# Gate logits taken from the attention rows by transposes on the chip, with the output's zero blocks and half of a weight load placed later

## The chip, the cores and the metric

The kernel runs on one core of a Trainium2 chip. The metric is the device time of one execution in microseconds (us). The core has TensorE (PE, its weight loads shown apart as PEld), VectorE (DVE), ScalarE (ACT), GpSimd (POOL) and SyncE (SP); 16 DMA engines move data between DRAM and the on-chip memories.

## What is computed

Local attention (8 batches, 8 heads, 576 positions, head size 64, each position sees itself and the 63 before it) gives 4608 rows of 512 numbers. A top-2 mixture of 8 experts works on these rows.

```
scores = q @ k.T / 8, masked to 0 <= i - j < 64
attn = exp(scores - max) / sum;   x = attn @ v          # 4608 rows of 512
logits = x @ w_gate;  noise_scale = log1p(exp(x @ w_noise))
noisy = logits + noise_scale * noise                    # 8 numbers a row
top 2 of noisy per row, softmax over the two
out[row] += weight * (relu(x[row] @ w1[e]) @ w2[e])     # for both experts e
```

All is in 32 bit floats; large products are split into high and low parts (three matmuls for one product).

## The kernel before

**Attention units.** The rows are made in 36 units of 128 rows (j = 0 to 35: position block j // 4, batch pair j % 4). One loop of 39 turns (j = 0 to 38) writes out, in each turn, the steps of several units, since the steps of one unit follow each other over turns: `scores` of unit j (16 matmuls into ps_s), `soft_a`, `soft_max`, `soft_max2` (a copy on ACT, a predicated copy and a maximum on DVE, a subtraction on POOL), then for j-1 `soft_b` (the exponential, ACT), `transp` (4 transposes on PE into ps_t) and `apply_mask` (DVE, makes pt), for j-2 `pv` (32 matmuls, 16 in the first four units, into ps_o) and for j-3 `norm_a` and `norm_b` (ACT scales ps_o by the reciprocal sum and writes the rows x). `store` sends the rows of j-4 to DRAM. Each engine works its instructions strictly in the written order, and SP issues all of these DMAs from one list, waiting where a transfer's buffer is not yet free or its data not yet made.

**The gate's logits before.** A logit is linear in v, so the kernel multiplies v by the gate weights first: `load_vt` brings v of unit j transposed (tile vt), `logits` makes 4 matmuls of 64 columns into the bank ps_g, and `logits_copy` (two ACT instructions) puts the result beside v in the tile vw. `pv` then has 85 columns a matmul (5 groups of 17: four with 16 numbers of v each, one with the 16 logits of the head; the 17th column of the first group holds the ones that give the sum), and `gate` adds over the heads on DVE, once for two units.

**Routing.** When a group of units has its logits (`ROUTE`: units 0-6, 7-13, 14-20, 21-26, 27-35), the generator `route` yields some 45 small steps on DVE and ACT; `drain(n)` takes n of them at five places in a turn (`RATE`). `slots` holds further steps (DVE, POOL line 592, and `place`, small matmuls that write into ps_o or ps_g), taken by `drain_slots`. From turn `TURN` on, the first rows of expert 0, gathered by POOL, are transposed by PE (line 726) into ps_t and split.

**After the attention.** `up00` is the first product of expert 0; 16 of its steps (`AHEAD`) run inside the turns 36 to 38, the rest right after. From there on the experts follow, `up` and `down` for 15 chunks of rows; `add_rows` adds their results to the output in DRAM. The output's 38 blocks of zeros (`zero_out`, 256 KB each) must be written before. Some stand in the turns from `ZFROM` on (`blanks`, three a turn), some later. `load_w2(0, ...)` brings expert 0's second weights in four pieces of 512 KB; `split_w2` splits them.

## Time and profile before

| | |
|---|---|
| median of 3 runs | 1014.37 us (1011.97 to 1015.88) |
| the profiled execution's own time | 1015.99 us |
| its span, first to last instruction | 1014.3 us |
| PE busy | 968.3 us (95%) |
| DVE / ACT / POOL busy | 692.7 / 524.0 / 319.2 us |
| mean granted TensorE clock | 0.993 of full speed |

Times below are positions or lengths in us in that span. The scores of unit 0 begin at 5.69, those of unit 4 at 20.25, of unit 11 at 54.29, of unit 32 at 150.38, of unit 35 at 172.92; the last matmul of `up00` begins at 201.78, and the products after it run until the end. A busy share is no bound by itself: which wait ends last in a stretch tells what sets its length.

### The profile page before, as it was taken

Reading aid. Unit: us, or ns where it says so; the run is one execution under the profiler, and the core shown is the slowest. Engines: PE = TensorE matmul, PEld = TensorE weight load, DVE = VectorE, ACT = ScalarE, POOL = GpSimd, SP = SyncE. Lnnn points to the kernel's source line nnn. Section 1 sums busy time; section 2 is a strip of 40 time slices with the busy share of each in tenths; the row PEclk is TensorE's granted clock in tenths of the full one; section 3 lists DMA queues with packets and bytes.
Section 4 is the critical chain, followed back from the end, with each engine's and each line's share of the span. In section 5 each row is a group of like instructions: output and inputs, shape, how many; then the busy total and the mean of one; then the engine's idle time right before and its main releaser. Section 6 shows DMA issues by size and latency. Waiting matters only on the chain.

```text
span 1014.3 us, 22006 instructions
## 1 busy us (share of the span) xinstructions
PE 968.3 (95%) x8464; PEld 868.4 (86%) x8464; DVE 692.7 (68%) x1727; ACT 524.0 (52%) x1346; POOL 319.2 (31%) x442
## 2 busy tenths in 40 slices
PE   8788887999999999999999999999999999999995
PEld 8677786888889898989898989888998899889994
DVE  5589897663676678667766776777577766776630
ACT  4788785522354445444554455445454545455420
POOL 5346554122322414141414141404141414131202
PEclk9999998999999999999999999999999999999998
DMA  9999999557558544855584558545854685465303
GB/s 327 334 294 315 290 287 325 184 137 230 138 140 209 97 129 97 227 113 128 100 251 85 128 113 231 106 115 121 241 96 106 127 234 108 97 147 147 47 3 52
DMA packets 107234, 168.93 MB, mean 167 GB/s; under 512 B 13360, under 2 KB 57648, under 8 KB 105328
## 3 DMA queue, kind: packets, MB, share of 16 engines
q1 hardware_dynamic: 89968, 126.96, 40.8%
q0 software_dynamic: 17152, 40.48, 22.7%
q8 instruction: 68, 1.11, 0.5%
q14 instruction: 46, 0.38, 0.1%
HBM read 110.08 MB, written 57.32 MB: 165 GB/s over the span
## 4 chain that ended last, share of the span: by engine, by line
PE 81%; DVE 9%; ACT 3%; issue 3%; POOL 2%; DMA 1%; POOLq 0%; DVEq 0%; ACTq 0%
PE ps_d L1025 8%; PE ps_d L1023 8%; PE ps_d L1024 8%; PE ps_z L879 6%; PE ps_z L881 6%; PE ps_z L880 6%; PE ps_v L879 3%; PE ps_v L880 3%; PE ps_v L881 3%; PE ps_y L1023 3%; PE ps_y L1025 3%; PE ps_y L1024 3%; DVE pt L359 2%; PE ps_y L881 2%; PE ps_y L880 2%
## 5 line engine op out<-in xcount | busy, mean ns | idle before, releaser
L957 POOL DMA_INDIRECT out_dram<-xg,los x70 | 110.3, 1576 | 396.9 <-ACT xg L1036 364.1
L1025 PE MATMUL ps_d<-w2h,hb 128*128 128x512 f32 x392 | 153.4, 391 | 0.0
L1023 PE MATMUL ps_d<-w2h,hb 128*128 128x512 f32 x392 | 153.3, 391 | 0.0
L1024 PE MATMUL ps_d<-w2l,hb 128*128 128x512 f32 x392 | 153.0, 390 | 0.0
L891 ACT ACTIVATE hb<-tq 128x288 fp32r<-128x288 f32 (+1 forms) x168 | 77.1, 459 | 144.2 <-DVE tq L910 144.2
L910 DVE TENSOR_TENSOR tq<-ps_z,tq 128x288 f32<-128x288 f32 (+1 forms) x168 | 79.4, 472 | 88.3 <-PE ps_z L881 88.0
L879 PE MATMUL ps_z<-xh,WH 128*128 128x288 f32 (+1 forms) x448 | 137.4, 307 | 1.1 <-DVE tq L910 0.2
L881 PE MATMUL ps_z<-xh,WL 128*128 128x288 f32 (+1 forms) x448 | 135.1, 302 | 0.0
L880 PE MATMUL ps_z<-xl,WH 128*128 128x288 f32 (+1 forms) x448 | 135.1, 302 | 0.0
L895 DVE SCALAR_TENSOR_TENSOR hb<-tq,hb 128x320 fp32r<-128x320 f32 (+2 forms) x168 | 75.6, 450 | 37.6 <-ACT hb L891 35.3
L690 POOL DMA_INDIRECT xg<-xrows,lxs x70 | 69.9, 999 | 87.6 <-DMA xs<-xg 33.8
L879 PEld LDWEIGHTS ps_z<-xh,WH 128*128 128x128 f32 x448 | 84.1, 188 | 5.9 <-DVE tq L910 4.2
L1025 PEld LDWEIGHTS ps_d<-w2h,hb 128*128 128x128 f32 x392 | 73.6, 188 | 15.9
L1024 PEld LDWEIGHTS ps_d<-w2l,hb 128*128 128x128 f32 x392 | 73.6, 188 | 14.1
L1023 PEld LDWEIGHTS ps_d<-w2h,hb 128*128 128x128 f32 x392 | 73.6, 188 | 14.0
L880 PEld LDWEIGHTS ps_z<-xl,WH 128*128 128x128 f32 x448 | 84.2, 188 | 1.3
L881 PEld LDWEIGHTS ps_z<-xh,WL 128*128 128x128 f32 x448 | 84.2, 188 | 0.0
L235 DVE TENSOR_TENSOR WL<-ws,WH 128x512 fp32r<-128x512 f32 x112 | 67.1, 614 | 6.4 <-ACT WH L243 6.4
L399 ACT ACTIVATE x<-ps_o,r 128x80 f32<-128x80 f32 x288 | 66.8, 349 | 8.7 <-DVE r L389 8.6
L774 ACT ACTIVATE xh<-tq 128x512 fp32r<-128x512 f32 (+1 forms) x70 | 42.7, 610 | 53.4 <-DVE tq L770 51.3
L378 PE MATMUL ps_o<-vw,pt 64*64 64x85 f32 x2176 | 50.9, 237 | 17.6 <-issue 12.7
L378 PEld LDWEIGHTS ps_o<-vw,pt 64*64 64x64 f32 x2176 | 45.8, 135 | 22.4 <-issue 13.9
(241 smaller groups left out, 2377.5 us busy)
## 6 DMA issues: line engine op xcount, KB each, us to landing
ws<-in_w_dram SPq DMA_DIRECT2D x14, 2048.0 KB, 11.5
xs<-xg SPq DMA_DIRECT2D x63, 256.0 KB, 3.3
vw<-in_vx_dram SPq DMA_DIRECT2D x36, 272.0 KB, 4.7
out_dram<-zero SPq DMA_DIRECT2D x38, 256.0 KB, 5.7
qc<-in_qT_dram SPq DMA_DIRECT2D x36, 256.0 KB, 5.2
KW<-in_kT_dram SPq DMA_DIRECT2D x36, 256.0 KB, 5.0
vt<-in_vT_dram SPq DMA_DIRECT2D x36, 256.0 KB, 4.6
xrows<-x SPq DMA_DIRECT2D x36, 256.0 KB, 4.6
```

The costliest lines, as they stand in the source:

```text
L378: nc.tensor.matmul(PO[j][u * 64:u * 64 + 64, a, g * 2 + x, :], lhsT=pt[pa, w, u * 2 + g, x * 64:x * 64 + 64], rhs=v[pa, (i + w) % 2, :, u, ...
L690: nc.gpsimd.indirect_dma_start(out=XG[e, c, q][:m], out_offset=None, in_=X[:DUMP + seen.get((e, c), NT) * 128], in_offset=bass.IndirectOff ...
L879: nc.tensor.matmul(p[:, :n], lhsT=WH[:, a, k, w], rhs=xh[:, b, k, :n], start=first and k == 0, stop=False, **free)
L880: nc.tensor.matmul(p[:, :n], lhsT=WH[:, a, k, w], rhs=xl[:, b, k, :n], start=False, stop=False, **free)
L881: nc.tensor.matmul(p[:, :n], lhsT=WL[:, a, k, w], rhs=xh[:, b, k, :n], start=False, stop=(k == 1), **free)
L891: nc.scalar.activation(hh[:, f, a:b], src, AF.Relu)
L895: nc.vector.scalar_tensor_tensor(hl[:, f, a:m], src[:, :m - a], 0.0, hh[:, f, a:m].bitcast(F32), op0=OP.max, op1=OP.subtract)
L910: nc.vector.tensor_tensor(t, a[:, :n], t, op=OP.add)
L957: s = nc.gpsimd.indirect_dma_start(out=out[:(2 + seen.get((e, c), NT)) * 128], out_offset=bass.IndirectOffsetOnAxis(ap=LT[e, c][1][q][:m], ...
L1023: nc.tensor.matmul(p, lhsT=h, rhs=w2h[:, f, :], **a)
L1024: nc.tensor.matmul(p, lhsT=h, rhs=w2l[:, f, :], start=False, stop=False)
L1025: nc.tensor.matmul(p, lhsT=l, rhs=w2h[:, f, :], **b)
```

## The change

The logits are now made from the finished rows. `turn_rows` transposes the 512 numbers of each row of unit j-4 on PE (4 transposes of 128x128 into ps_g), `rows_copy` copies them by one ACT instruction to the new tile xq, and `logits` in the next turn makes 4 matmuls of 16 columns, one accumulation, into a free part of a ps_o bank; `gate` is a copy of 16 columns on DVE in each turn. The loads of vt, the line `logits_copy` and four POOL memsets of vw are gone; `pv` has 65 columns, and vw's load is 260 KB instead of 272 KB (the array of v is laid out anew by the host, with 64 numbers and a one for each head). `gate` comes two units later than before. For the last units a table (`LATE`) packs the remaining transposes and logits into turns 36 to 38 and behind the loop.

Zero blocks start at turn 36 instead of 32: 9 stand in the loop, 9 and 12 in the first `up` and `down` of expert 0, 8 in its second `up`. Expert 0's second weights are loaded in turns 35 to 38 instead of 34 to 37. `RATE` is 9 steps a turn instead of 8 and 7, `drain_slots` takes three a turn throughout, `TURN` is 33, and 14 steps of `up00` stand in the loop, 2 more behind it.

```diff
@@ -36,7 +36,7 @@
 W1G = 12
-TURN = 32
+TURN = 33
@@ -44,10 +44,10 @@
-ZFROM = 32
+ZFROM = 36
 HOLD = 4
-RATE = ((16, 8), (99, 7))
+RATE = ((99, 9),)
@@ -128,21 +128,13 @@
         i, bp = divmod(j, NP)
-        nc.sync.dma_start(VW[bp][:, i % 2, 0:4], vx[bp, i])
-    def load_vt(j):
-        i, bp = divmod(j, NP)
-        VT[j] = ld.tile([128, 4, 128], F32, name="vt", bufs=2)
-        nc.sync.dma_start(VT[j], vT[bp, i])
+        nc.sync.dma_start(VW[bp][:, i % 2], vx[bp, i])
         load_qk(j)
-    wgx_sb = acon.tile([128, 2, 64], F32)
+    wgx_sb = acon.tile([128, 4, 2 * E], F32)
     nc.sync.dma_start(wgx_sb, wgx)
-    load_vt(0)
     load_v(0)
-    load_vt(1)
@@ -181,8 +173,6 @@
     nc.vector.tensor_scalar(maskT[:, 1], maskT[:, 0], -1.0, 1.0, op0=OP.mult, op1=OP.add)
-    for v in VW:
-        nc.gpsimd.memset(v[:, :, 4], 0.0)
@@ -277,22 +267,22 @@
-    VG = idle[:, 0:256].rearrange("p (n c) -> p n c", n=1)
-    def logits(j):
-        p = VG[:, 0]
-        x = VT.pop(j)
-        for u in range(2):
-            for g in range(2):
-                q = u * 2 + g
-                nc.tensor.matmul(p[:, q * 64:q * 64 + 64], lhsT=x[:, q, :], rhs=wgx_sb[:, g], start=True, stop=True)
-    def logits_copy(j):
-        i, bp = divmod(j, NP)
-        for a in range(2):
-            h = slice(a * 64, a * 64 + 64)
-            nc.scalar.activation(VW[bp][h, i % 2, 4, :, :, 0:16].rearrange("p u (g x) e -> p (u g) x e", x=2),
-                                 VG[h, 0].rearrange("p (k a x e) -> p k a x e", a=2, x=2, e=16)[:, :, a], AF.Copy)
+    XQ, LP = {}, {}
+    def turn_rows(j):
+        x = XT[j]
+        for q in range(4):
+            nc.tensor.transpose(idle[:, q * 128:q * 128 + 128], x[:, q].rearrange("p h d -> p (h d)"), ident)
+    def rows_copy(j):
+        XQ[j] = wk.tile([128, 4, 128], F32, name="xq")
+        nc.scalar.activation(XQ[j], idle.rearrange("p (q t) -> p q t", q=4), AF.Copy)
+    def logits(j, o):
+        LP[j] = o[:, 0, 352 + j % 4 * 2 * E:352 + (j % 4 + 1) * 2 * E]
+        x = XQ.pop(j)
+        for q in range(4):
+            nc.tensor.matmul(LP[j], lhsT=x[:, q], rhs=wgx_sb[:, q], start=(q == 0), stop=(q == 3))
@@ -367,7 +357,7 @@
         OT[j] = o
-        PO[j] = o[:, :, 0:340].rearrange("p a (k d) -> p a k d", d=85)
+        PO[j] = o[:, :, 0:260].rearrange("p a (k d) -> p a k d", d=65)
@@ -377,7 +367,7 @@
                                              lhsT=pt[pa, w, u * 2 + g, x * 64:x * 64 + 64],
-                                             rhs=v[pa, (i + w) % 2, :, u, g * 2 + x, :],
+                                             rhs=v[pa, (i + w) % 2, u, g * 2 + x, :],
@@ -385,24 +375,24 @@
         RS[j] = r
-        nc.scalar.activation(r, PO[j][:, :, :, 16], AF.Copy, bias=1e-9)
+        nc.scalar.activation(r, PO[j][:, :, :, 64], AF.Copy, bias=1e-9)
             if j % 2 == 0:
-                XP[0] = wk.tile([128, 2, 5, H, 16], F32, name="x", bufs=2)
+                XP[0] = wk.tile([128, 2, 4, H, 16], F32, name="x", bufs=2)
             XT[j] = XP[0][:, j % 2]
-        o, r = PO[j][:, a].rearrange("p k (q d) -> p k q d", d=17), RS[j][:, a]
+        o, r = PO[j][:, a, :, 0:64].rearrange("p k (q d) -> p k q d", d=16), RS[j][:, a]
         for k in range(4):
-            nc.scalar.activation(XT[j][:, :, a * 4 + k], o[:, k, :, 0:16], AF.Copy, scale=r[:, k:k + 1])
+            nc.scalar.activation(XT[j][:, :, a * 4 + k], o[:, k], AF.Copy, scale=r[:, k:k + 1])
         nc.sync.dma_start(X[DUMP + j * 128:DUMP + (j + 1) * 128, :DM],
-                          XT.pop(j)[:, 0:4].rearrange("p q h d -> p (q h d)"))
-    LG, PG, held = {}, {}, []
+                          XT[j].rearrange("p q h d -> p (q h d)"))
+    LG, PG = {}, {}
@@ -410,12 +400,7 @@
             LG[c] = gw.tile([128, RT, 16], F32, name="lg", bufs=3)
-        held.append(j)
-        if j % 2 or j + 1 == ROUTE[c + 1]:
-            a = held[0] % 2
-            nc.vector.tensor_reduce(LG[c][:, held[0] - ROUTE[c]:j + 1 - ROUTE[c]],
-                                    XP[0][:, a:a + len(held), 4].rearrange("p n h e -> p n e h"), op=OP.add, axis=AX.X)
-            held.clear()
+        nc.vector.tensor_copy(LG[c][:, j - ROUTE[c]], LP.pop(j))
@@ -628,7 +613,7 @@
     def place_slots(j):
-        o = OT.pop(j)[:, 0, 340:340 + E * NQ]
+        o = OT[j][:, 0, 264:264 + E * NQ]
@@ -1069,7 +1054,7 @@
         for _ in range(n):
-            if j >= NT and len(taken) < AHEAD:
+            if j >= NT and len(taken) < AHEAD - (0 if kept else 2):
@@ -1089,6 +1074,9 @@
             zero_out()
+    kept = []
+    LATE = {NT: ([NT - 5], [NT - 4], []), NT + 1: ([], [NT - 3], [NT - 2]), NT + 2: ([NT - 2], [], [NT - 1])}
@@ -1101,8 +1089,8 @@
             load_v(j + 2)
-        if NT - 2 <= j < NT + 2:
-            load_w2(0, slice((j - NT + 2) * 2, (j - NT + 3) * 2))
+        if NT - 1 <= j < NT + 3:
+            load_w2(0, slice((j - NT + 1) * 2, (j - NT + 2) * 2))
@@ -1119,6 +1107,12 @@
         on(place_slots, j - 2)
+        ready = LATE[j][0] if j in LATE else [j - 5]
+        for k in ready:
+            on(logits, k, OT[min(j, NT + 1) - 2] if j > 1 else None)
+        if j == NT + 1:
+            turn_rows(j - 4)
+            rows_copy(j - 4)
@@ -1127,23 +1121,31 @@
             add_slots(placed.pop())
+        for k in ready:
+            on(gate, k)
         ahead(2)
-        on(logits, j)
-        if j < NT - 2:
-            load_vt(j + 2)
+        if j <= NT:
+            on(turn_rows, j - 4)
         drain(rate(2))
-        on(logits_copy, j)
+        if j <= NT:
+            on(rows_copy, j - 4)
         ahead(2)
-        on(gate, j - 3)
+        if j in LATE:
+            for k in LATE[j][1]:
+                logits(k, OT[min(j, NT + 1) - 2])
+                gate(k)
+            for k in LATE[j][2]:
+                turn_rows(k)
+                rows_copy(k)
         drain(rate(3))
-        drain_slots(2 if j >= DENSE else 1 + j % 2)
+        drain_slots(2)
@@ -1151,6 +1153,10 @@
     store(NT - 1)
+    kept.append(1)
+    ahead(2)
+    logits(NT - 1, OT[NT - 1])
+    gate(NT - 1)
@@ -1173,6 +1179,7 @@
             parts.append((0.0, 1.0, [lambda: drain_slots(1)] * 9))
+            parts.append((0.0, 0.8, [zero_out] * 9))
@@ -1218,6 +1225,7 @@
             parts.append((0.1, 0.96, [lambda: drain(2)] * 24))
+            parts.append((0.0, 0.9, [zero_out] * 12))
```

PE's list in a late turn, before (ps_s scores, vw v, ps_t transposed probabilities, vt transposed v, xg gathered rows of expert 0; the small matmuls of `place` are left out):

```order
L318 MATMUL ps_s<-KW,qc 64x128 x16
L378 MATMUL ps_o<-vw_93,pt 64x85 x32
...
L354 MATMUL ps_t<-ident,p 128x128 x4
L288 MATMUL ps_g<-wgx_sb,vt 128x64 x4
L726 MATMUL ps_t<-ident,xg 128x128 x4
```

Such a turn with the change (lines 275 and 285 are `turn_rows` and `logits`; x the finished rows, xq their transposed copy):

```order
L308 MATMUL ps_s<-KW,qc 64x128 x16
L368 MATMUL ps_o<-vw_90,pt 64x65 x32
...
L285 MATMUL ps_o<-wgx_sb,xq 128x16 x4
L344 MATMUL ps_t<-ident,p 128x128 x4
L275 MATMUL ps_g<-ident,x 128x128 x4
L711 MATMUL ps_t<-ident,xg 128x128 x4
```

The logits moved from behind the transposes of the probabilities to ahead of them, and four transposes of rows came in behind.

PE's list from the last `pv` on, before (WH, WL and xh are weights and rows of `up00`):

```order
L378 MATMUL ps_o<-vw_93,pt 64x85 x32
L836 MATMUL ps_t<-xh,WH 128x384
L837 MATMUL ps_t<-xl,WH 128x384
L838 MATMUL ps_t<-xh,WL 128x384
...
L608 MATMUL ps_g<-xc 128x80
```

With the change:

```order
L368 MATMUL ps_o<-vw_93,pt 64x65 x32
L275 MATMUL ps_g<-ident,x 128x128 x4
L821 MATMUL ps_t<-xh,WH 128x384
...
L285 MATMUL ps_o<-wgx_sb,xq 128x16 x4
L275 MATMUL ps_g<-ident,x 128x128 x4
L821 MATMUL ps_s<-xh,WH 128x384
```

Behind the last `pv` three more sets of transposes and three of logits now stand between the steps of `up00` (those of units 33, 34 and 35).

SP's list at the end of the attention, before (xrows<-x is `store`, xrows<-xc the gate weights of the last group, ws the staged expert weights):

```order
L219 DMA ws<-in_w_dram 128x1024
L199 DMA out_dram<-zero 256x1x256 x2
L402 DMA xrows<-x 128x512
L199 DMA out_dram<-zero 256x1x256 x3
L579 DMA xrows<-xc 128x9x16
L199 DMA out_dram<-zero 256x1x256 x8
L215 DMA ws<-in_w_dram 128x4096
L199 DMA out_dram<-zero 256x1x256 x9
```

With the change:

```order
L209 DMA ws<-in_w_dram 128x1024
L189 DMA out_dram<-zero 256x1x256 x2
L392 DMA xrows<-x 128x512
L189 DMA out_dram<-zero 256x1x256 x21
L564 DMA xrows<-xc 128x9x16
L189 DMA out_dram<-zero 256x1x256 x8
L205 DMA ws<-in_w_dram 128x4096
```

21 blocks now stand in a row behind the last store and ahead of the last gate weights.

## Rows read from the trace of the kernel before

**Rows 1.** Stretches of the span: length, busy time (instructions) of each engine, clock, DMA share, GB/s
```profile
0.00:20.25 20.25, 17.92 (x288) 16.67 (x288) 10.57 (x23) 6.61 (x19) 12.74 (x42) 1.00 0.90 315
20.25:54.29 34.04, 25.90 (x694) 23.78 (x693) 20.60 (x33) 27.73 (x104) 12.19 (x15) 1.00 0.99 337
54.29:150.38 96.09, 83.19 (x2323) 75.15 (x2322) 87.75 (x219) 79.23 (x304) 55.32 (x64) 1.00 0.94 295
150.38:172.92 22.54, 15.81 (x356) 14.11 (x356) 17.41 (x42) 12.58 (x46) 12.86 (x15) 0.93 1.03 359
172.92:201.95 29.03, 26.81 (x353) 25.21 (x352) 19.66 (x62) 16.93 (x58) 2.24 (x3) 0.94 0.55 184
201.95:1014.00 812.05, 798.66 (x4458) 713.50 (x4457) 536.76 (x1350) 380.89 (x819) 223.84 (x306) 1.00 0.58 135
```

**Rows 2.** The chain of work that ended last: start, length, what
```profile
2.28 1.06 POOL vw L185 x4
12.28 0.84 PE ps_g L288 x8
...
24.15 1.08 PE ps_s L318 x32
27.97 1.08 PE ps_s L318 x32
```

**Rows 3.** PE in order of time: start, length, instruction, count [idle before <- releaser]
```profile
13.05 0.69 PE L320 MATMUL ps_s<-KW,qc 64*64 64x64 f32 x32
13.56 0.81 PE L378 MATMUL ps_o<-vw,pt 64*64 64x85 f32 x32
...
35.05 1.11 PE L378 MATMUL ps_o<-vw,pt 64*64 64x85 f32 x48 [1.67 <-issue]
36.09 0.66 PE L354 MATMUL ps_t<-ident,p 128*128 128x128 f32 x4
36.58 1.00 PE L288 MATMUL ps_g<-wgx_sb,vt 128*128 128x64 f32 x8
37.51 1.10 PE L318 MATMUL ps_s<-KW,qc 64*64 64x128 f32 x32
38.44 0.89 PE L378 MATMUL ps_o<-vw,pt 64*64 64x85 f32 x35
40.65 0.81 PE L378 MATMUL ps_o<-vw,pt 64*64 64x85 f32 x29 [1.32 <-issue]
...
47.38 0.51 PE L378 MATMUL ps_o<-vw,pt 64*64 64x85 f32 x11 [2.44 <-issue]
```

**Rows 4.** DMA issues of the page: kind, count, size, median us to landing
```profile
out_dram<-zero SPq DMA_DIRECT2D x38, 256.0 KB, 5.7
vt<-in_vT_dram SPq DMA_DIRECT2D x36, 256.0 KB, 4.6
```

**Rows 5.** Groups of instructions between 54 and 150 us: count | busy, mean ns | idle before
```profile
L378 PE MATMUL ps_o<-vw,pt 64*64 64x85 f32 x1344 | 29.7, 235 | 7.6 <-issue 3.0 <-ACT t L328 1.7 <-DVE xc L539 1.0
L328 ACT ACTIVATE t<-ps_s 128x512 f32<-128x512 f32 x21 | 12.5, 594 | 4.4 <-PE ps_s L318 4.0 <-PE ps_g L469 0.4
L294 ACT ACTIVATE vw<-ps_g 64x128 f32<-64x128 f32 x42 | 11.5, 275 | 1.6 <-PE ps_g L288 1.3
L416 DVE TENSOR_REDUCE lg<-x 128x32 f32<-128x256 f32 (+1 forms) x13 | 6.5, 500 | 0.0
L389 DVE RECIPROCAL r<-r 128x8 f32<-128x8 f32 x21 | 4.1, 196 | 1.6 <-ACT r L388 1.6
L628 DVE TENSOR_TENSOR SLOT<-SLOT,ps_o 128x80 f32<-128x80 f32 x8 | 1.8, 227 | 0.0
```

**Rows 6.** PE in order of time, 150 to 184 us, columns as in the third group
```profile
157.53 0.66 PE L726 MATMUL ps_t<-ident,xg 128*128 128x128 f32 x4 [1.35 <-DVE pt L359]
...
169.03 0.37 PE L378 MATMUL ps_o<-vw,pt 64*64 64x85 f32 x6 [2.71 <-issue]
...
172.92 1.99 PE L318 MATMUL ps_s<-KW,qc 64*64 64x128 f32 x32
174.68 2.27 PE L378 MATMUL ps_o<-vw,pt 64*64 64x85 f32 x64
```

More of the change, by code (lines that the diff above doesn't have):

```diff
@@ L88, in tile_kernel @@
 @with_exitstack
-def tile_kernel(ctx, tc, qT, kT, vx, vT, wgx, noise, w1, w2, out):
+def tile_kernel(ctx, tc, qT, kT, vx, wgx, noise, w1, w2, out):
     nc = tc.nc
@@ L110, in tile_kernel @@
     KW = acon.tile([128, NP, 2, H, 64], F32)
-    VW = [acon.tile([128, 2, 5, 2, 4, 17], F32, name=f"vw{j}") for j in range(NP)]
-    QC, VT = {}, {}
+    VW = [acon.tile([128, 2, 2, 4, 65], F32, name=f"vw{j}") for j in range(NP)]
+    QC = {}
     def load_q(j):
@@ L1290, in tile_kernel @@
                 overflow(e, k)
-_INS = {"qT": [NP, 128, NB, H, 64], "kT": [NP, 128, NB, H, 64], "vx": [NP, NB, 128, 4, 2, 4, 17],
-        "vT": [NP, NB, 128, 4, 128], "wgx": [128, 2, 64], "noise": [128, NT, E], "w1": [E, 128, KD, F], "w2": [E, 128, KF, DM]}
+_INS = {"qT": [NP, 128, NB, H, 64], "kT": [NP, 128, NB, H, 64], "vx": [NP, NB, 128, 2, 4, 65],
+        "wgx": [128, 4, 2 * E], "noise": [128, NT, E], "w1": [E, 128, KD, F], "w2": [E, 128, KF, DM]}
 def layout(inputs):
@@ L1302, in heads @@
         return np.ascontiguousarray(a.transpose(0, 1, 5, 3, 2, 4)).reshape(NP, 128, NB, H, 64)
-    v = inputs["v"].reshape(NP, 2, 2, 2, 2, NB, 64, 4, 16)
-    vx = np.zeros((NP, NB, 2, 64, 4, 2, 2, 2, 17), np.float32)
-    vx[..., :16] = v.transpose(0, 5, 2, 6, 7, 1, 3, 4, 8)
-    vx[:, :, :, :, 0, :, :, :, 16] = 1.0
-    vT = v.reshape(NP, 2, 2, 2, 2, NB, 64, D).transpose(0, 5, 4, 7, 1, 3, 2, 6).reshape(NP, NB, 128, 4, 128)
-    wg = np.concatenate([inputs["moe_w_gate"], inputs["moe_w_noise"]], axis=1).reshape(2, 2, 2, 64, 16)
-    wgx = np.zeros((2, 64, 2, 2, 2, 16), np.float32)
-    for x in range(2):
-        wgx[x, :, :, :, x] = wg[:, :, x].transpose(2, 1, 0, 3)
+    v = inputs["v"].reshape(NP, 2, 2, 4, NB, 64, D)
+    vx = np.ones((NP, NB, 2, 64, 2, 4, 65), np.float32)
+    vx[..., :64] = v.transpose(0, 4, 2, 5, 1, 3, 6)
+    wg = np.concatenate([inputs["moe_w_gate"], inputs["moe_w_noise"]], axis=1).reshape(H, 4, 16, 2 * E)
+    wgx = wg.transpose(0, 2, 1, 3)
     noise = inputs["moe_noise"].reshape(NP, 2, NB, 64, E).transpose(1, 3, 2, 0, 4).reshape(128, NT, E)
@@ L1322, in layout @@
     w2 = inputs["moe_w2"].reshape(E, KF, 128, DM).transpose(0, 2, 1, 3)
-    a = dict(qT=heads(inputs["q"]), kT=heads(inputs["k"]), vx=vx.reshape(_INS["vx"]), vT=vT,
+    a = dict(qT=heads(inputs["q"]), kT=heads(inputs["k"]), vx=vx.reshape(_INS["vx"]),
              wgx=wgx.reshape(_INS["wgx"]), noise=noise, w1=w1, w2=w2)
```

## The prediction

> **What bounds the kernel now.** I read the busy times by stretch first, then the chain of waits, then PE's instructions in order of time, then the groups of the middle stretch. The stretches are cut at starts of scores: units 0 to 3, 4 to 10, 11 to 31, 32 to 34, then the rest up to the first output product of expert 0, and all behind it [rows 1]. In the last stretch PE is busy 798.66 of 812.05 us, and its products are not touched; the change can act on the first 201.95 us only. There no engine is full. PE is busy 17.92 of the first 20.25 us, and the chain runs over its logits and scores [rows 1, 2]. Units 4 to 10 take 34.04 / 7 = 4.86 us each with PE busy 25.90 and the DMA engines at 0.99; their loop on the chain is 3.82 us (27.97 - 24.15), and what is over holds three PE stalls of 1.67, 1.32 and 2.44 us that wait for nothing shown [rows 1 to 3]. Units 11 to 31 take 96.09 / 21 = 4.58 us each, and DVE is busy 87.75 of 96.09, 91%: DVE is nearest to being the bound, PE (83.19) comes next. Units 32 to 34 take 22.54 / 3 = 7.51 us each, with the DMA share at 1.03 and a granted clock of 0.93 [rows 1].
>
> **Prices on PE.** From start to start [rows 3]: four transposes take 0.49 us (36.09 to 36.58), the logits 0.93 (36.58 to 37.51), the scores 0.93 (37.51 to 38.44), 48 of 64 pv records 1.04 (35.05 to 36.09), so a whole pv 1.39. A pv of 65 columns has no row: 32 records of 64 columns took 0.51 (13.05 to 13.56), which makes 1.02 for 64 records, the lower bound; a straight line through 85 columns (0.0217 us a record) and the scores' 128 columns (0.029) gives 0.0183, so 1.17, the upper one. I take 1.06, near the 64 column row. Logits with 16 columns have no row either. They keep 4 weight tiles of 128x128, each in two records: the upper bound is the present 0.93; the lower is the transposes' 0.49, which load 4 such tiles too. I take 0.93, because 64 columns already cost 0.116 a record while the transposes' 128 columns cost 0.123, so the columns hardly count. A steady unit then needs 0.93 + 1.06 + 0.93 + 0.49 + 0.49 = 3.90 us of PE, where it needed 0.93 + 1.39 + 0.49 + 0.93 = 3.74: 0.16 more, and still below 4.58.
>
> **Prices elsewhere.** ACT loses two copies of 275 ns a unit and gains one of 128x512 out of PSUM, as the 594 ns of line 328 [rows 5]: 0.04 us more, between nothing and its own 0.59 if the removed copies only filled waits. It is hidden behind DVE's work: ACT is busy 79.23 of 96.09; without that cover it costs 0.04 a unit, 1.5 us in all. DVE loses 6.5 us of reduces in units 11 to 31 and gains 21 copies of 128x16: between the reciprocal's 196 ns (half the numbers) and the 227 ns of line 628 (five times the numbers, out of PSUM) I take 210, so 4.4 us [rows 5]. DMA: the vt load of 256 KB goes [rows 4], vw's shrinks by 12 KB, 268 KB a unit.
>
> **Term 1, units 0 to 3.** Four POOL memsets of 1.06 us in the first chain go; three sets of logits on the chain (units 1 to 3) go, since now the first logits come in turn 5: 3 x 0.93 = 2.8 [rows 2, 3]. Between 1.1 (the memsets alone, if the softmax takes PE's place) and 4.1 (all, with pv's saving): I take -3.3.
>
> **Term 2, units 4 to 10.** PE's 3.90 us take the place of the loop's 3.82: no gain there. The stalls are another matter. Between the first and the second PE ran 48 + 4 + 8 + 32 + 35 = 127 records, each with its weight load, about 254 instructions; the stalls come at a fixed count of instructions, not at a step of the kernel [rows 3]. I read them as late delivery of instructions, with the DMA engines full at 337 GB/s [rows 1]. Seven units now move 7 x 268 KB = 1.92 MB less of 34.04 us x 337 GB/s = 11.5 MB; at that rate they need 28.3 us, so up to 5.7 can go. Zero if delivery stays as late. I take -3.5. On this the Trainium skill, "Runtime: NRT & Kernel Launch", section "Instruction fetch mechanics", says that instructions come by DMA in blocks of 256 and that this is mostly hidden. The count of the trace agrees with the blocks; the three stalls, 5.43 us, do not agree with hidden. By the page's "hidden" this term would be 0, and the sum 3.5 us higher.
>
> **Term 3, units 11 to 31.** DVE -6.5 + 4.4 = -2.1. PE's stalls without a shown cause ahead of pv are 3.0 us there [rows 5]; I let 1 go. Together -3.1. Down to -6 if all go. Upwards: the transposes of the probabilities stand behind the logits now, 0.93 - 0.33 = 0.60 us later in each unit. Behind them waits DVE's line 359, and behind that the next pv. Today DVE arrives there late (busy 91%), which hides it; uncovered for 8 of 21 units it costs 5 us. Route steps are only taken earlier (9 a turn), not added.
>
> **Term 4, units 32 to 34.** The 2.71 us stall at 166.3 falls into a stretch at 359 GB/s, in which 12 zero blocks and the first pieces of w2 are sent [rows 1, 6]; these blocks go, and so do the loads of vt. Behind the stall the granted clock falls (0.93 over the stretch): from 169.03 to 172.92, 3.9 us for work of about 2.6 (0.1 + 0.15 + 0.49 + 0.93 + 0.49 + 0.27). The wait of 1.35 us for ps_t in front of the expert's transposes stays, one unit later. 2.7 + 1.3 = 4.0, and half a us of smaller stalls: -4.5; from 0 (the stall stays, and with it the clock) to -6.
>
> **Term 5, unit 35 to the output products.** What left the start comes back here: 5 sets of logits (units 31 to 35; the old 35th leaves) and 5 sets of transposes, 5 x 0.93 + 5 x 0.49 = 7.1, less three pv of 0.33: +6.1. The slow clock at 172.92 goes: scores took 1.76 (to 174.68) instead of 0.93, and the pv behind it, 2.2 instead of 1.39, so -1.65 [rows 3, 6]. Each of the last transposes waits for ACT's normed rows and each logits for ACT's copy of 0.59, with 6 PE records between: +1 for these, -1 for waits that the new work fills. +4.5; from +2 to +7.
>
> **Term 6, behind that.** 21 zero blocks in a row (SP waits for nothing between them) are 5.5 MB, 16 us at 337 GB/s, beside the first output products. The last store and the last piece of w2 stand ahead of them. 0, up to +3 if gathers for the next chunk come late.
>
> **The sum.** -3.3 - 3.5 - 3.1 - 4.5 + 4.5 + 0 = -9.9. The profiled execution took 1015.99 us (span 1014.3), so 1006.1; it lies 1.6 above the median of the runs, 1014.37, which gives **1004.5 us**. All lower bounds together: -4.1 - 5.7 - 6 - 6 + 2 = -19.8; all upper: -1.1 + 0 + 5 + 0 + 7 + 3 = +13.9.
>
> **Rivals.** (a) *Nothing to be had:* the stalls and the clock's fall stay where they are, since PE takes as many instructions as before: terms 2 and 4 are 0, term 3 the DVE's -2.1. -3.3 - 2.1 + 4.5 = -0.9: 1013.5. For it: stalls also occur where the DMA engines carry 295 GB/s (units 11 to 31). Against it: they are largest where the engines are full. The page's "hidden" points here as well. (b) *PE's order becomes the loop:* the 0.60 us by which the transposes of the probabilities come later reach DVE in every one of the 21 units: +12.6 - 2.1. With the other terms at -3.3, -3.5, -4.5, +4.5: +3.7; with term 2 at 0 too, since the same delay binds there: +7.2, 1021.6. It decides from where PE's 3.90 us and its waits pass the present 4.58, so from 0.68 us of waits a unit. For it: PE's idle time is 12.9 us in those units, 0.61 each, so it is close. Against it: part of that idle time is waiting for DVE, which does not add. (c) *All DMA relief arrives:* terms 2 to 4 at their lower ends: -3.3 - 5.7 - 6 - 6 + 4.5 = -16.5: 998. For it: the DMA share of 0.94 to 1.03 all along.
>
> **Chances.** The forecast (about 1000 to 1009) 0.45, (a) 0.24, (b) 0.14, (c) 0.17. 0.5% (5.1 us) is about what a measurement of this kernel can tell from no change. Faster by more than that, below 1009.3: 0.45 + 0.17 = 0.62; within: 0.24; slower: 0.14. The range reaches from the lower end of (c), 995, into (b) as far as 1017, and leaves out about 0.2; the forecast's own is 1000 to 1009.
>
> **What would show it.** Right: units 4 to 10 near 4.3 us each and a DMA share below 0.95; DVE still above 90% in units 11 to 31 at about 4.4 us; a clock of 1.00 throughout 150 to 200; no zero block before the last five units; six sets of logits behind the last scores. Wrong: line 349 (the old 359) on DVE waiting for the transposes of ps_t in most units, stalls of PE as long as before, or waits on ACT's rows and copies in the last units of more than 2 us.

## The result and the profile after

The changed kernel took 1019.06 us (median of 18 runs, 1013.65 to 1021.68), the kernel before 1012.81 (18 runs): a ratio of 1.0051, 95% interval 1.0040 to 1.0063. The forecast was 1004.5, the range ended at 1017: the time lies outside, on the other side of no change. The profiled execution took 1020.64 us, with a span of 1018.9 and a mean granted clock of 0.987 (0.993 before). The profiled execution of the kernel before, 1015.99 us, lies 3.2 us above its median of these runs, that of the changed kernel 1.6 above its own: a difference between the two profiles is one between two executions, and is checked below against further ones.

Busy times by stretch of the changed kernel, columns and cuts as in [rows 1] (busy shares in the order PE, PEld, DVE, ACT, POOL, then clock, DMA share and GB/s); the last two rows are pieces of the fifth stretch:

```profile
0.00:17.69 17.69, 14.39 (x257) 12.75 (x257) 8.48 (x22) 4.26 (x11) 10.64 (x37) 1.00 0.87 295
17.69:49.32 31.63, 28.34 (x713) 25.67 (x712) 19.98 (x36) 25.84 (x95) 13.40 (x16) 0.95 0.95 314
49.32:145.11 95.79, 88.05 (x2407) 79.14 (x2406) 86.93 (x225) 78.00 (x284) 52.18 (x60) 1.00 0.76 230
145.11:165.57 20.46, 16.28 (x353) 14.56 (x353) 16.27 (x43) 12.21 (x43) 16.48 (x19) 0.83 0.58 197
165.57:206.95 41.38, 37.09 (x427) 34.20 (x427) 20.45 (x69) 19.00 (x59) 3.00 (x3) 0.88 0.72 230
206.95:1018.90 811.95, 798.64 (x4458) 713.35 (x4457) 536.83 (x1350) 381.62 (x822) 223.76 (x306) 1.00 0.57 133
...
173.00:192.50 19.50, 17.06 (x224) 15.65 (x224) 8.99 (x39) 8.54 (x32) 0.00 (x0) 0.92 0.62 188
192.50:200.10 7.60, 7.56 (x33) 7.25 (x34) 1.44 (x6) 1.61 (x3) 0.00 (x0) 0.55 1.02 354
```

| stretch | before | after | difference | predicted |
|---|---|---|---|---|
| units 0 to 3 | 20.25 | 17.69 | -2.56 | -3.3 |
| units 4 to 10 | 34.04 | 31.63 | -2.41 | -3.5 |
| units 11 to 31 | 96.09 | 95.79 | -0.30 | -3.1 |
| units 32 to 34 | 22.54 | 20.46 | -2.08 | -4.5 |
| unit 35 to the first output product | 29.03 | 41.38 | +12.35 | +4.5 |
| behind it, to the end of the span | 812.35 | 811.95 | -0.40 | 0 |

In these two executions the first four stretches all won, though less than forecast; the fifth lost more than they won. In it PE is busy 37.09 us where it was 26.81 [rows 1], and its clock is 0.88. PE in order of time shows three places of the changed kernel (columns as in [rows 3]):

```profile
156.68 1.11 PE L711 MATMUL ps_t<-ident,xg 128*128 128x128 f32 x4 [2.54 <-DVE pt L349]
157.72 1.99 PE L308 MATMUL ps_s<-KW,qc 64*64 64x128 f32 x32
...
170.97 0.66 PE L711 MATMUL ps_t<-ident,xg 128*128 128x128 f32 x4 [0.88 <-DVE pt L349]
172.31 0.45 PE L821 MATMUL ps_s<-xh,WH 128*128 128x384 f32 x1 [0.69 <-ACT xh L716]
173.04 0.69 PE L822 MATMUL ps_s<-xl,WH 128*128 128x384 f32 x1 [0.28 <-DVE xl L717]
...
192.54 0.66 PE L275 MATMUL ps_g<-ident,x 128*128 128x128 f32 x4 [2.04 <-ACT x L389]
...
193.73 0.52 PE L821 MATMUL ps_s<-xh,WH 128*128 128x384 f32 x1
194.05 0.52 PE L822 MATMUL ps_s<-xl,WH 128*128 128x384 f32 x1
...
200.27 0.34 PE L823 MATMUL ps_z<-xh,WL 128*128 128x384 f32 x1
200.45 0.35 PE L821 MATMUL ps_z<-xh,WH 128*128 128x384 f32 x1
```

The products of `up00` start every 0.32 us at 193.73 and every 0.17 us from 200.27 on. Between, PE has no wait: it works at the lower of its two clock levels (1.2 and 2.4 GHz; the mean over 192.5 to 200.1 is 0.55), after a wait of 2.04 us. The same happens behind the wait of 2.54 us: the scores at 157.72 take 1.99 us, where they took 1.10 [rows 3]. The wait at 192.54 is on ACT, whose list is in order:

```profile
188.57 0.60 ACT L279 ACTIVATE xq<-ps_g 128x512 f32<-128x512 f32 x1 [0.80 <-PE ps_g L275]
189.06 0.17 ACT L378 ACTIVATE r<-ps_o 128x8 f32<-128x8 f32 x1
190.39 0.93 ACT L389 ACTIVATE x<-ps_o,r 128x64 f32<-128x64 f32 x4 [1.16 <-PE ps_o L285]
191.56 0.93 ACT L389 ACTIVATE x<-ps_o,r 128x64 f32<-128x64 f32 x4 [0.24 <-DVE lg L403]
```

The norms of unit 35 stand behind `rows_copy` of unit 34, which waits for PE's transposes, and then behind logits written into the same bank of ps_o. So two theories: **clock**, PE's waits near the end and the slow stretches behind them; **work**, the sets of logits and transposes behind the last scores. A third, the **traffic** of the zero blocks, has the DMA share of 1.02 in the slow stretch for it.

### The profile page after: what moved, and what is told of

It reads as the page before. It is cut to its first block, busy times and chain, and to the rows that moved or that the text cites. A ratio compares the mean times of both kernels' runs of the same rounds, so it can differ in the third digit from the quotient of the medians.

```text
span 1018.9 us, 22209 instructions
## 1 busy us (share of the span) xinstructions
PE 982.8 (96%) x8608; PEld 879.7 (86%) x8608; DVE 688.9 (68%) x1742; ACT 520.9 (51%) x1310; POOL 319.5 (31%) x438
## 4 chain that ended last, share of the span: by engine, by line
PE 75%; DVE 2%; issue 1%; ACT 1%; POOL 0%; POOLq 0%; DVEq 0%; ACTq 0%
PE ps_d L1010 8%; PE ps_d L1008 8%; PE ps_d L1009 8%; PE ps_z L864 6%; PE ps_z L866 6%; PE ps_z L865 6%; PE ps_v L864 3%; PE ps_v L865 3%; PE ps_v L866 3%; PE ps_y L1010 2%; PE ps_y L1008 2%; PE ps_y L1009 2%; PE ps_y L865 2%; PE ps_y L866 2%; PE ps_y L864 2%; PE ps_d L1014 1%
## 5 line engine op out<-in xcount | busy, mean ns | idle before, releaser
L389 ACT ACTIVATE x<-ps_o,r 128x64 f32<-128x64 f32 x288 | 63.0, 334 | 10.6 <-DVE r L379 9.2
L739 DVE STREAM_TRANSPOSE tq<-xc 128x256 f32<-128x256 f32 (+1 forms) x140 | 52.0, 409 | 18.0 <-DMA xc<-xs 16.7
L233 ACT ACTIVATE WH<-ws 128x512 fp32r<-128x512 f32 (+1 forms) x112 | 60.0, 568 | 0.0
```

## The experiments at the end of the attention

An idle matmul below is one of `ones` by `ones`, 128 columns, about 0.25 us, into a part of ps_o that nobody reads. Ratios are to the kernel before, run beside it on the same chip.

**Filling one wait.**

```diff
+            if j == NT + 2:
+                for _ in range(8):
+                    nc.tensor.matmul(OT[NT - 2][:, 1, 384:512], lhsT=ones, rhs=ones, start=True, stop=True)
             for k in LATE[j][2]:
                 turn_rows(k)
```

> The changed kernel with 8 idle matmuls of 128x128 by 128 columns on PE right ahead of turn_rows(35) in turn 38, into a bank that nothing reads: they stand where PE waits 2.04 us for unit 35's rows, and take nothing else away. Theory 'clock': PE does not rest there, the granted clock stays at the higher level from 192 to 200, and the time is 2 to 3.5 us below that of the changed kernel (the wait stays, filled). Rival 'work': the added matmuls cost 0 to 1 us or change nothing. If the clock stays high and the time does not move, the theory falls too.

1016.17 us, ratio 1.0031 (1.0012 to 1.0051), 2.9 us below the changed kernel's median. Eight matmuls that compute nothing seem to have made it faster, which is for the clock, but the intervals of the two ratios still overlap. PE in its profile (line 1146 is the filling):

```profile
158.06 1.11 PE L711 MATMUL ps_t<-ident,xg 128*128 128x128 f32 x4 [2.54 <-DVE pt L349]
159.11 1.99 PE L308 MATMUL ps_s<-KW,qc 64*64 64x128 f32 x32
...
192.74 2.02 PE L1146 MATMUL ps_o<-ones 128*128 128x128 f32 x16
194.94 0.66 PE L275 MATMUL ps_g<-ident,x 128*128 128x128 f32 x4 [0.17 <-ACT x L389]
...
195.61 0.33 PE L822 MATMUL ps_s<-xl,WH 128*128 128x384 f32 x1
195.78 0.34 PE L823 MATMUL ps_s<-xh,WL 128*128 128x384 f32 x1
```

Behind the filled wait the products start every 0.17 us, with a clock of 1.00 from 193 to 200; behind the wait of 2.54 us, which is not filled, the scores still take 1.99. The DMA share from 193 to 200 is 0.98, so the traffic alone does not lower the clock.

**Removing that wait.** In turn 37 the norms of unit 35 go ahead of the transposes of unit 34 (and leave their place in turn 38), and the last logits go to unit 34's bank:

```diff
+            if j == NT + 1:
+                norm_a(NT - 1)
+                norm_b(NT - 1, 0)
+                norm_b(NT - 1, 1)
             for k in LATE[j][2]:
...
-                logits(k, OT[min(j, NT + 1) - 2])
+                logits(k, OT[NT - 2])
```

> The changed kernel with two things altered: the norms of unit 35 (norm_a, norm_b) are written ahead of turn_rows(34) and rows_copy(34) in turn 37, and the logits of units 33 to 35 go into unit 34's ps_o bank instead of unit 35's. Theory 'clock' (PE's waits of some 2 us near the end, each followed by a stretch at the lower clock, make most of the +12.35 us between the scores of unit 35 and the first output product): the wait of 2.04 us at 192.5 falls below 0.8 us, the stretch 193.4 to 200.0 runs at full clock, and the time is 3.5 to 5 us below that of the changed kernel, near 1014.5 to 1015.5. Rival 'work' (six sets of transposes and logits behind the last scores cost what they cost on PE, the clock is a side matter): the wait may go, but at most 2 us come back, 1017 or more.

1018.76 us, ratio 1.0063 (1.0046 to 1.0080): no gain, against the clock theory's number. In its profile the wait of 2.04 became waits of 1.11 and 0.40 us, with slow products again behind them (0.32 us from start to start at 190.26). Moving a wait is no cure. The same profile has an exception: behind the wait of 2.54 us, which the edit does not touch, the scores take 1.10 us.

```profile
156.89 0.66 PE L711 MATMUL ps_t<-ident,xg 128*128 128x128 f32 x4 [2.54 <-DVE pt L349]
157.47 1.10 PE L308 MATMUL ps_s<-KW,qc 64*64 64x128 f32 x32
```

So a wait of this length is not followed by the slow clock in every execution.

**Leaving out the last three sets** (`turn_rows`, `rows_copy` and `logits` return at once for units 33 to 35).

> The changed kernel without the transposes, copies and logits of units 33, 34 and 35 (their gate logits are set to 0, so these rows go to other experts than they should). It leaves out 3 sets of PE work, 3 x (0.91 + 0.49) = 4.2 us by the trace, and with them the waits for ACT's rows. Theory 'work': 4 to 5 us below the changed kernel, near 1014.5. Theory 'clock': the wait of 2.04 us and the low clock behind it go too, so 4.2 + 2.0 + 3.3 = 7 to 9.5 us below, near 1010 to 1012. Work behind 207 changes a little since other rows are chosen; the first output product's start tells more than the time.

1012.25 us, ratio 0.9994 (0.9973 to 1.0015): 6.8 below the changed kernel, just short of what the clock theory gave. The stretch from unit 35 on:

```profile
161.96:192.85 30.89, 28.64 (x392) 26.10 (x391) 17.84 (x65) 16.96 (x56) 1.71 (x2) 1.00 0.73 233
```

That is 10.5 us less than 41.38, with a clock of 1.00, for 4.2 us of work; behind it, where other rows are chosen, the kernel takes 1.8 us more.

**TURN back at 32.** Only `TURN = 33` becomes 32.

> The changed kernel with TURN back at 32: the first rows of expert 0 are transposed and split (line 711, 716, 717) one turn earlier. In the changed kernel's last turn with scores PE waits 0.88 us in front of these transposes and 0.69 + 0.28 us in front of the first steps of up00, and 5 of the transposes stand behind the scores of unit 35. Theory 'a turn too late': these waits and 0.9 us of work leave the stretch from unit 35's scores to the first output product, which shrinks by 2 to 2.7 us, units 32 to 34 take up to 1 us more, and the time falls by 1 to 2.5 us against the changed kernel's 1019.06 us. Rival 'logits and transposes alone': the time stays within 1 us.

1020.54 us, ratio 1.0063 (1.0043 to 1.0082): not the gain expected. But the stretches show why:

```profile
50.90:152.25 101.35, 91.65 (x2407) 81.63 (x2406) 87.68 (x225) 77.97 (x284) 57.30 (x65) 0.98 0.76 235
...
173.04:208.20 35.16, 32.74 (x423) 30.91 (x423) 19.75 (x67) 18.37 (x58) 3.00 (x3) 0.95 0.81 259
```

The last stretch fell by 6.2 us; units 11 to 31 lost 5.6, which the edit doesn't touch. PE there, in one pv while POOL's gathers run (143.83 to 147.6):

```profile
145.12 0.39 PE L368 MATMUL ps_o<-vw,pt 64*64 64x65 f32 x7 [0.48 <-issue]
145.92 0.34 PE L368 MATMUL ps_o<-vw,pt 64*64 64x65 f32 x4 [0.41 <-issue]
146.67 0.29 PE L368 MATMUL ps_o<-vw,pt 64*64 64x65 f32 x2 [0.41 <-issue]
```

Such stalls stand in the profiles of all four kernels that ran on this chip (this one and the three told of below with "the stalls by the gathers") and in no other, so their times can't be set beside the others', only their stretches. Why the stalls came on that chip stays open.

**All waits filled**, and beside it the changed kernel unaltered:

```diff
+    FILL = {33: 9, 34: 3, 35: 3}
...
+        for _ in range(FILL.get(j, 0)):
+            nc.tensor.matmul(OT[j - 2][:, 1, 384:512], lhsT=ones, rhs=ones, start=True, stop=True)
         for f in aux.get(j, ()):
```

and 3 ahead of `up00`, 8 ahead of `turn_rows(35)`.

> The changed kernel itself, unaltered, as the yardstick for the others of this call: the profiles of the kernels so far show a group of short PE stalls around 146 to 149 us, while POOL's gathers run, in four kernels and none in five others, so it may belong to the chip and the execution rather than to the edits. If it belongs to the execution: the unaltered kernel can show it too, and its time is 1015 to 1022 us. If it belongs to the edits: it does not show here.

> The changed kernel with idle matmuls (128x128 by 128 columns, two records and about 0.25 us each) in every longer wait of PE's near the end: 9, 3 and 3 ahead of the expert's transposes of turns 33 to 35 (waits of 2.54, 0.92 and 0.88 us), 3 ahead of the first step of up00, 8 ahead of turn_rows(35) (2.04 us). They remove no wait and add up to 1 us of work. Theory 'clock': the granted clock stays at its higher level from the scores of unit 32 to the first output product, units 32 to 34 take 17 to 18 us, the last stretch 36.5 to 38, and the time is 4 to 6 us below the unaltered kernel of the same call. Rival 'work': within 1 us of it, or slower by the added work.

> TURN back at 32 and idle matmuls in its waits: 4, 7 and 6 ahead of the expert's transposes in turns 32 to 34 (0.99, 1.78 and 1.68 us) and 8 ahead of turn_rows(35). Theory 'clock and a turn too late together': the last stretch falls to 33 to 34 us at full clock (35.16 at 0.95 without the fill), units 32 to 34 to 18.5 to 19.5, and the time is 1 to 2 us below that of the kernel with the fills alone. Rival 'the waits only move': what the last stretch wins units 32 to 34 lose, and the time is that of the fills alone within 1 us.

Unaltered: 1018.61 us, 1.0046 (1.0025 to 1.0067), no stalls by the gathers. All filled: 1014.27, 1.0009 (0.9992 to 1.0026), 4.3 us less. With TURN 32 as well: 1010.93, 0.9978 (0.9961 to 0.9994), another 3.3 less. The mean clocks over 12 runs each were 0.989, 0.995 and 0.994. Units 32 to 34 and the stretch behind, with all filled:

```profile
143.70:162.02 18.32, 16.56 (x377) 14.91 (x376) 15.97 (x43) 12.19 (x43) 15.94 (x19) 1.00 0.59 201
162.02:199.04 37.02, 35.49 (x455) 33.17 (x455) 20.33 (x69) 19.01 (x59) 3.68 (x4) 1.00 0.74 235
```

and with TURN 32 as well:

```profile
145.28:164.28 19.00, 17.90 (x391) 16.43 (x391) 16.73 (x45) 12.69 (x44) 15.98 (x19) 1.00 0.60 202
164.28:198.12 33.84, 33.27 (x439) 31.38 (x439) 19.67 (x67) 18.41 (x58) 3.66 (x4) 1.00 0.80 255
```

The clock is 1.00 in all four rows, as the theory demands. 41.38 - 37.02 = 4.4 us of the last stretch are the clock's; against the unaltered kernel's profile beside it, where the stretch took 39.94 us at a clock of 0.91, they are 2.9. 37.02 - 33.84 = 3.2 are the late turn's (0.7 of them paid back in units 32 to 34), and 33.84 is 4.8 over before.

> The version e10 unaltered, as the yardstick of this call and to see its gain a second time: ratio to before 0.996 to 0.9995 if the gain is real, 1.000 or more if the first measurement was luck.

The version with TURN 32 once more, on another chip: 1010.44, 0.9995 (0.9977 to 1.0014), with 33.81 us in the last stretch. It beats the changed kernel by about 8 us, the kernel before by 0.2% at most, and the second measurement can't be told from no gain at all.

**The same cure for the kernel before** (`FILL = {32: 5, 33: 4, 34: 2}`).

> The kernel before with idle matmuls (128x128 by 128 columns) in front of the expert's transposes of turns 32, 33 and 34: 5, 4 and 2, where PE waits 1.35, 0.94 us and nothing. Theory 'the clock hits before less': before's fall of the clock stands behind the stall of 2.71 us, in which PE waits for nothing shown and which no idle matmul can fill, so the time stays within 1.5 us of before. Rival 'the same cure': the time falls by 3 us or more, as the changed kernel's did, and the change is no gain against it.

1012.36 us, 0.9997 (0.9982 to 1.0012): nothing to win. Units 32 to 34 and the last stretch in its profile:

```profile
151.69:170.86 19.17, 16.80 (x379) 15.22 (x378) 17.22 (x42) 12.37 (x46) 12.84 (x15) 1.00 1.01 352
170.86:198.87 28.01, 25.22 (x355) 23.48 (x353) 19.48 (x62) 16.76 (x58) 2.22 (x3) 1.00 0.72 236
```

So at the higher clock the change costs 37.02 - 28.01 = 9.0 us in the last stretch, and 33.84 - 28.01 = 5.8 with TURN 32; in units 32 to 34 it wins 0.85.

## The experiments in the middle

**Routing at the old rates** (`RATE = ((16, 8), (99, 7))`, `drain_slots(2 if j >= DENSE else 1 + j % 2)`; with these the output is not the right one, so only the middle is read).

> The changed kernel with the routing steps taken as before (RATE 8, then 7 a turn; drain_slots by turns 1 and 2 until unit 24). Units 11 to 31 took 95.79 us with DVE busy 86.93, where the reduces that went and the copies that came make 6.5 - 3.5 = 3.0 us less than before's 87.75. Theory 'routing steps drawn forward': DVE falls to about 85 in that stretch, which shortens by 1.5 to 2.5 us, and the steps come back at the end, up to as much. Rival 'PE has become the loop': PE, busy 88.05 there, sets the length, DVE falls and the stretch stays within 0.7 us.

1026.66 us, 1.0124 (1.0100 to 1.0148), with the stalls by the gathers. DVE's busy time in the third stretch is 83.86 us, 3.1 less. But from the scores of unit 11 to those of unit 31, ahead of the gathers, it took 137.98 - 46.80 = 91.2 us, where the changed kernel took 140.89 - 49.32 = 91.6. Three microseconds less on DVE are worth 0.4 at most (the unaltered kernel's second profile has 91.4 itself): DVE does not set the length.

**Transposes of the probabilities ahead of the logits** (which are taken from behind `place_slots`).

```diff
         on(transp, j - 1)
+        for k in ready:
+            on(logits, k, OT[min(j, NT + 1) - 2] if j > 1 else None)
```

> The changed kernel with each unit's logits written behind the transposes of the probabilities instead of ahead of them (the gate's copy then behind apply_mask). Rival (b) of the prediction (the transposes of the probabilities come 0.9 us later in each unit and DVE waits for them): units 11 to 31 shorten by 2 us or more, units 4 to 10 by up to 1. Theory 'PE's list is full, whatever its order': units 11 to 31 stay within 1 us of 95.79 and DVE's wait for ps_t only becomes another wait.

1025.29 us, 1.0122 (1.0097 to 1.0146). Units 11 to 30 took 147.09 - 49.13 = 98.0 us, 6.4 more. The order that rival (b) blamed is the better one.

**A quarter of the logits' products in units 8 to 27** (`n = 1 if 8 <= j < 28 else 4`, a loop over n; three quarters of these rows' sums are left out).

> The changed kernel with one of the four logits products in units 8 to 27 (three quarters of the sum over the rows' numbers is left out there, so these rows go to other experts): 6 PE records, 0.69 us, less a unit, and nothing else in the loop changes. Theory 'PE has become the loop of units 11 to 31': 17 of the 21 units lose up to 0.69 us, and the stretch shortens by 5 us or more from 95.8. Rival 'DVE sets it' (86.93 of 95.79 us busy): it shortens by less than 2 us. Both can hold in turn in different units: then 2 to 5.

1015.61 us, 1.0024 (1.0005 to 1.0043), 3.0 below the changed kernel beside it, though the intervals of the two ratios overlap. The third stretch, 95.63 us in that one:

```profile
48.31:140.60 92.29, 76.49 (x2293) 66.78 (x2292) 85.66 (x225) 77.06 (x284) 51.31 (x59) 1.00 0.79 237
```

11.5 us less on PE gave 3.3. So neither engine bounds the stretch alone: PE sets the length of some units (a unit took as little as 3.41 us, 3.88 in the changed kernel). That waits across engines set that of the others is argued, not shown.

## The experiments on the traffic

Units 4 to 10 differ from execution to execution, so one profile tells little here. Four profiles of kernels with the old order there took 30.95 to 34.04 us (mean 32.8), eleven with the new order, whose instructions in these units are the same, 28.95 to 35.17 (mean 31.7), at clocks of 0.90 to 1.00. The two extremes of the new order:

```profile
17.67:52.84 35.17, 30.16 (x714) 27.19 (x713) 19.96 (x36) 25.80 (x95) 13.38 (x16) 0.90 0.87 283
17.67:46.62 28.95, 26.58 (x714) 24.00 (x713) 19.80 (x36) 25.69 (x95) 13.41 (x16) 1.00 0.97 327
```

**A load kept**, in the changed kernel and in the version with TURN 32 and the filled waits:

```diff
+        if j < NT - 2:
+            i, bp = divmod(j + 2, NP)
+            dm = ld.tile([128, H, 64], F32, name="dm", bufs=2)
+            nc.sync.dma_start(dm, qT[bp, :, i])
         on(norm_b, j - 3, 1)
```

> The changed kernel with a load of 256 KB a unit added back where vt's was (it reads q again, and nothing reads what it brings). The prediction's term 2 put -3.5 us in units 4 to 10 down to the traffic that went; measured were -2.4 in the profiled runs. Theory 'traffic': units 4 to 10 go back to 33 to 34 us with stalls of 1.3 to 2.5 us that wait for nothing shown, and the time rises by 1.5 to 3 us over the changed kernel's 1019.06. Rival 'PE's own': units 4 to 10 stay within 0.7 us of what they take without the load, and the time within 1 us.

> The version with TURN 32 and the filled waits (1010.93 us, ratio to before 0.9978), with a load of 256 KB a unit added back where vt's was (it reads q again, and nothing reads what it brings). Theory 'traffic' (prediction's term 2): units 4 to 10 lose their gain, 33 to 34 us, and units 11 to 31 up to 2 us, so ratio to before 1.000 to 1.005. Rival 'traffic is worth nothing': ratio to before within 0.0015 of 0.9978.

In the changed kernel 1025.31 us, 1.0108 (1.0069 to 1.0148), but with the stalls by the gathers: inconclusive. In the other 1014.29, 1.0021 (1.0007 to 1.0036), where it was 0.9978 and, once more, 0.9995: 0.3 to 0.4% slower, and the second interval overlaps. Units 4 to 10 took 32.62 and 32.74 us, both within the spread above; the second has stalls of 0.77 and 2.71 us.

PE's stalls without a shown cause are shorter with less traffic. From the scores of unit 11 to those of unit 31 those of 0.2 us and more sum to 3.9 to 5.3 us in four profiles with the old order (DMA share 0.90 to 0.95), to 0.5 to 2.5 in ten with the new one (0.74 to 0.77), and to 4.1 and 1.7 in the two with the load kept (0.91), so the load alone brings them back clearly in one of the two. They cost little there: with the load these units took 91.83 us in the version with TURN 32 and the filled waits, without it 91.89; in the changed kernel 93.19 and 91.57.

**Weights later**: in the version with TURN 32 and the filled waits, expert 0's first weights loaded in turns 9 to 16 instead of 2 to 9 (`W1G = 26`); their splits on POOL and ACT move with them.

> The version with TURN 32 and the filled waits (e10), with expert 0's first weights loaded in turns 9 to 16 instead of 2 to 9 (W1G 26 instead of 12; POOL's and ACT's splits of them move by 7 turns too). The loads that leave turns 4 to 8 are 5 of 256 KB. Theory 'traffic delays the instructions': units 4 to 10 take 28 to 29.5 us at a clock of 0.98 or more, without a stall over 1 us, units 11 to 31 within 1 us of 96, and the time is 1.5 to 3 us below e10's. Rival 'the stalls come with the instruction count whatever the traffic': units 4 to 10 stay at 30 to 33 us, or the stalls move into units 9 to 16; time within 1 us.

1017.42 us, 1.0051 (1.0031 to 1.0071), where that version beside it had 0.9995: slower, by 7 us. Units 4 to 10 and 11 to 31:

```profile
17.70:45.67 27.97, 26.59 (x713) 24.01 (x712) 19.39 (x36) 23.75 (x87) 7.77 (x8) 1.00 0.91 287
45.67:151.52 105.85, 94.33 (x2406) 84.56 (x2406) 92.28 (x225) 80.23 (x291) 57.63 (x68) 0.94 0.73 228
```

Units 4 to 10 took 27.97 us, the least of any profile, and their longest stall without a shown cause was 0.48 us, where it was 0.78 to 2.18 in the eleven above. This fits instructions that come in time with less traffic, from one profile; the splits that left these units with the loads are a rival that it does not exclude. Units 11 to 31 took 105.85 us, in the run beside it 95.90: from 83.13 to 110.63 the clock is 0.75, and moved splits run there. Whether they are the cause is not shown.

**Transfers moved alone, moved back, moved with filled waits.** `ZFROM`, the turns of `load_w2` and the two lists of `zero_out`:

> The kernel before with only the transfers moved as in the change: zero blocks from turn 36 on, 9 and 12 of them in expert 0's first up and down, the second weights one turn later. The prediction's term 4 read the 2.71 us stall and the clock's fall behind it in units 32 to 34 as caused by these transfers: then units 32 to 34 take 3 to 4.5 us less and the time is 2 to 4 us below before, near 1009 to 1011. Rival: the stall stays or another wait takes its place, the time is that of before within 1.5 us. Rival 'late blocks': the 21 blocks in a row or the late weights delay the products of expert 0, slower than before by 1 to 4 us, shown as waits behind 205.

> The version with TURN 32 and the filled waits, with zero blocks from turn 32 on and the second weights in turns 34 to 37, as before the change. Theory 'late transfers help units 32 to 34' (prediction's term 4): the stretch shows a stall of 1.3 to 2.7 us that waits for nothing shown and a lower clock behind it, and the time is 2 to 4 us above 1010.93 (ratio to before 0.9998 to 1.002). Rival 'worth nothing or late': ratio 0.996 to 0.998.

> The kernel before with the filled waits of the run e12 and the transfers moved as in the change. If the 2.71 us stall comes from these transfers, then with both away the clock stays at its higher level from 150 to 202 and the time is 3 to 5 us below before (ratio 0.995 to 0.997): then the on-chip logits bring nothing beside it. Rival: the stall of 1.3 us stays as it did with the transfers moved alone, ratio 0.998 to 1.001.

Into before: 1013.76 us, 1.0014 (0.9996 to 1.0031). Into before with filled waits: 1016.90, 1.0042 (1.0024 to 1.0060), where it was 0.9997. Taken back in the version with TURN 32 and the filled waits: 1012.59, 1.0008 (0.9991 to 1.0024), where it was 0.9978 and 0.9995. So the move harms the old order where the waits are filled, by 0.45%; that it helps the new one is not clear of the noise. With the blocks back at turn 32 stalls are back (PE of that run; the DMA share of units 32 to 34 is 1.00):

```profile
165.76 0.72 PE L1154 MATMUL ps_o<-ones 128*128 128x128 f32 x5 [1.16 <-issue]
172.59 0.33 PE L344 MATMUL ps_t<-ident,p 128*128 128x128 f32 x1 [1.77 <-issue]
```

But the stalls do not hang on the blocks alone. Moved into before, units 32 to 34 took 19.17 us at a clock of 1.00, without the 2.71 us stall; the kernel before with filled waits, whose blocks are at turn 32, took 19.17 as well (above), and its longest stall there is 1.73. With the move and filled waits one of 2.36 stands behind the scores of unit 32, with a DMA share of 1.03 from 150 to 154, and the clock of units 32 to 34 is 0.85:

```profile
154.01 1.39 PE L378 MATMUL ps_o<-vw,pt 64*64 64x85 f32 x26 [2.36 <-issue]
```

In that kernel DVE also waits 5.74 us, by its profile for a zero block, and PE's small matmul of `place` behind it 5.35:

```profile
198.85 0.56 DVE L847 SCALAR_TENSOR_TENSOR hb<-ps_z,hb 128x384 fp32r<-128x384 f32 x1 [5.74 <-DMA out_dram<-zero]
200.21 0.42 PE L608 MATMUL ps_g<-xc 128*128 128x80 bf16 x4 [5.35 <-DVE SLOT L628]
```

In the changed kernel DVE waits 3.15 us for a zero block (at 201.28); PE has 9 us more of its own to do at that place, and shows no such wait.

## Why the prediction was wrong

**Term 5 is the step that failed:** +4.5 forecast, +12.35 measured. Three parts of it, by the runs with filled waits:
- The work itself was right: +6.1 forecast, and at the higher clock in both, with TURN 32, the stretch is 33.84 - 28.01 = 5.8 us longer.
- *The turn* was not in the term. The prediction knew that the expert's transposes came "one unit later", and counted it in term 4 alone as a wait that stays. One set of these transposes, with the waits of 0.88, 0.69 and 0.28 us, moved behind the last scores, where PE is busy 35.49 of 37.02 us with the waits filled: 3.2 us.
- *The clock* had the wrong sign. "The slow clock at 172.92 goes", at -1.65, took the fall to hang on one stall. The term did see the waits on ACT's rows, but priced them "+1 for these, -1 for waits that the new work fills": their length. Behind the wait of 2.04 us stand 7.6 us at a clock of 0.55, which is 3.4 us lost; by the runs with filled waits 2.9 to 4.4 in the stretch. What would show the prediction wrong was named ("waits on ACT's rows and copies in the last units of more than 2 us"); no rival had it with a price.

**Term 4** (-4.5, measured -2.08) took one execution's stall and fall of the clock for a property of the kernel before. With the waits filled the stretch takes 18.32 us, -4.2 against the 22.54 of that profile; but the kernel before at a clock of 1.00 takes 19.17, with its blocks at turn 32, and against that it is -0.85. The blocks can make stalls, as the run with the transfers back shows; that the 2.71 us were theirs is not shown. In the changed kernel a wait of 2.54 us for DVE's line 349 stands there, with a slow stretch behind it in this execution. The term also added its work up as "about 2.6" where its parts make 2.43.

**Term 3** (-3.1, measured -0.30) took DVE for the bound from its share of 91%. DVE won only 0.8 us, since routing steps came forward; and had it won 3.1 more, the stretch would have gained 0.4. The stalls ahead of pv did go, from 3.0 us to 0.8, more than the 1 us that was counted. Against them stands PE's work, 88.05 us where it was 83.19, which the prediction held to be hidden; by the run with a quarter of the products a microsecond of it is worth 3.3 / 11.5 = 0.29 here, so some 1.4 us, an estimate. Rival (b), whose 1021.6 lies near the measured time, gave it for another reason: its place was in units 11 to 31, which were not slower.

**Term 2** (-3.5, measured -2.41) has its mechanism supported, but not its size: over all profiles the means differ by 1.0 us, with spreads of 3 and 6, and the lower clock of the stretch (0.95, 1.00 before) takes part of any gain. The instructions are themselves in the DMA trace: the kernel before from 164 to 170 us, where the stall of 2.71 us stands [rows 6] (queue, packets, MB, share of 16 engines):

```profile
q1 hardware_dynamic: 1321, 1.89, 100.1%
q8 instruction: 1, 0.02, 1.0%
```

One packet of instructions among 1321 of data. Over the whole run that queue moved 68 packets, 1.11 MB, so 16 KB each. The Trainium skill, "Runtime: NRT & Kernel Launch", section "Instruction fetch mechanics", says that each sequencer fetches blocks of 16 KiB through a DMA queue of its own, and that this is mostly hidden. The trace agrees with the blocks. With "hidden" it agrees in units 11 to 30 of the changed kernel (stalls of 0.85 us in 91.57), and not in units 4 to 10 of the kernel before (5.43 in 34.04).

**Terms 1 and 6** held: -2.56, the same to 0.04 us in all profiles, and no change behind the first output product (811.95 us, 812.35 before).

The span grew by 4.6 us where -9.9 was forecast. Of these 14.5 us the clock is 4.4 + 2.1, the turn 3.2, term 3 2.8, terms 1 and 2 1.8: 14.3. This adds up two executions; in the medians, filling the waits gave 4.3 us back and the turn another 3.3.
